# Loads of four heads' q and k put ahead of the decay rows, two heads' values behind them, and six more filler matmuls

## The chip, the cores and the metric

The kernel runs on one core of a Trainium2 chip. The core has five engines that take their instructions from queues of their own: TensorE (PE; its weight loads are listed apart as PEld), VectorE (DVE), ScalarE (ACT), GpSimd (POOL) and SyncE (SP). Transfers are issued from an engine's queue, most of them here from POOL's and the rest from SP's, and run on 16 DMA engines that all of the core's queues share. The metric is the device time of one execution in microseconds (us), as the median of several runs.

## What is computed

Eight batches of eight heads of causal attention with forget gates, 576 positions of 64 elements each; the heads are then joined to 512 columns and go through a two-layer network with the activation h - tanh(h).

```python
def _attn_ref(q, k, v, f):                      # q, k, v: (8, 8, 576, 64); f: (8, 8, 576)
    scale = 1.0 / np.sqrt(D)
    scores = scale * np.matmul(q, k.transpose(0, 1, 3, 2))
    log_f = np.log(np.clip(f, 0.0001, 1.0))
    cum = np.cumsum(log_f, axis=-1)
    decay = cum[:, :, :, None] - cum[:, :, None, :]
    causal = np.triu(np.ones((S, S), dtype=bool), k=1)
    scores = np.where(causal, -1000000000.0, scores + decay)
    scores = scores - np.max(scores, axis=-1, keepdims=True)
    attn = np.exp(scores)
    attn = attn / (np.sum(attn, axis=-1, keepdims=True) + 1e-09)
    return np.matmul(attn, v).astype(np.float32)

def _moe_ref(x, w_in, w_out):                   # x: (4608, 512); w_in: (512, 2048); w_out: (2048, 512)
    h = x @ w_in
    g = h - np.tanh(h)
    return (g @ w_out).astype(np.float32)
```

## The kernel before, in words

The order of each engine's instructions is the order in which the program emits them. The work goes in 32 pairs of heads (`pairs`: batch b, pair c of four), and the network's work (`mlp`) is mixed in from the fifth pair on.

A pair goes through these steps. `trans` (line 287) turns q and then k of both heads on PE by six transposes each into one PSUM bank, and two copies by DVE or ACT carry them to `QT` and `KT` (lines 309 and 311). `scores` (line 337) makes the products of k and q for seven tiles, `ti` 0 to 6 (matmuls of line 352; in batch 0 a second matmul of line 355 adds the causal mask `late`); ACT takes the exponential (line 361) out of one of a few PSUM banks: two of `ps_sc`, and for some tiles the one of `ps_tr`. `values` (line 382) multiplies the exponentials by v (matmuls of line 389), DVE divides (lines 398 to 400) and `turn` brings the result to `XR` (line 417), from which the network reads.

The decay is put into the score product: `QT` and `KT` have 67 rows each, 64 of the head and three more, the decay rows, which hold the running sum of log f in two parts (`chi`, `clo`) and constants. DVE makes `chi` (line 189) and `clo` (line 190) from the running sum of line 187. Head 0's rows are written by engines (lines 191 and 572). Those of heads 1 to 7 of batch 0 come by three DMAs on POOL's queue, which `bulk` issues: `k_hi` (line 211), `q_hi` (line 212) and `k_lo` (line 213). The first use of the rows is in pair 0 (heads 0 and 1): tile `ti` 3 has a matmul for each of its two heads, and tiles 4 to 6 belong to head 1.

POOL's queue in batch 0, in order: the identity (line 147); q, k, q, k of heads 0 to 3, two heads in each (`load_qk`, line 102); then the last 64 positions of v for all heads (`load_v_rest`, line 123) and the other 512 positions of heads 0 and 1 (`load_v_head`, line 127), from lines 166 to 168; the mask `late` (line 169); and then `bulk`: the three decay rows' DMAs, q, k, q, k of heads 4 to 7 (lines 214 to 217), and v of heads 2 to 7 in four blocks (`load_v_block`, line 131). After that come the loads for batch 1 and the weights, at places that `LOADS` (line 228) names.

PE's order around this: 47 filler matmuls, then `trans` of pair 0 with more filler between (`start`, line 570), tiles 0 and 1 of pair 0, two fillers; then from `att_items` (line 591) for p = 0: `trans` of pair 1's q, tile 2, six fillers, tile 3, `trans` of pair 1's k, tile 4, tile 5, four fillers, tile 6, six fillers. For p = 1 follow tile 0 of pair 1, `trans` of pair 2's q, tile 1, `trans` of pair 2's k, tile 2, `values` of pair 0's head 0, tiles 3 and 4, `values` of pair 0's head 1, and so on. The fillers are made by `unread` (line 563): matmuls of a constant into a PSUM bank (`ps_tr`, or one that is lent) that nothing reads.

Of the kernel before, what the change touches and what calls it, by code (L numbers as in the profile page):

```python
# [21 lines left out]
def kernel(  # L22
# [13 lines left out]
    B, H, S, D = q.shape  # L36
# [56 lines left out]
    qn, kn = ([t[0:S // NT6, :].rearrange("p (h n d) -> p h n d", h=H, n=NT6) for t in raw] for raw in (qraw, kraw))  # L93
# [7 lines left out]
    def load_qk(dst, src, b, h0, h1):  # L101
        nc.gpsimd.dma_start(  # L102
            out=dst[b % 2][:, h0:h1, :, :].rearrange("p h n d -> p h (n d)"),
            in_=src[b, h0:h1, :, :].rearrange("h (p n) d -> p h (n d)", n=NT6))
# [17 lines left out]
    def load_v_rest(b):  # L122
        nc.gpsimd.dma_start(out=vn[b % 2][0:S % P, NJ - 1, :, 0:D],
                            in_=v[b, :, S - S % P:S, :].rearrange("h p d -> p h d"))

    def load_v_head(b, h):
        nc.gpsimd.dma_start(out=vn[b % 2][:, 0:NJ - 1, h, 0:D],  # L127
                            in_=v[b, h, 0:S - S % P, :].rearrange("(n p) d -> p n d", p=P))

    def load_v_block(b, n, h0, h1):  # L130
        nc.gpsimd.dma_start(out=vn[b % 2][:, n, h0:h1, 0:D],  # L131
                            in_=v[b, h0:h1, n * P:(n + 1) * P, :].rearrange("h p d -> p h d"))
# [30 lines left out]
    nc.vector.memset(vn[0][D:P, NJ - 1, :, :], 0.0)  # L163
    mul_k, add_k, mul_l, mul_q, add_q, both = (per[:, i:i + 1] for i in range(6))
    EL = [cst.tile([P, 192], FP16, tag=f"el{i}", name=f"el{i}") for i in range(3)]
    load_v_rest(0)
    load_v_head(0, 0)
    load_v_head(0, 1)
    nc.gpsimd.affine_select(out=late, in_=late, compare_op=ALU.is_ge, fill=-60000.0,
                            base=0, pattern=[[1, P]], channel_multiplier=-1)  # L170

    r_hi, r_one = (id16[0:NX, NH + g:NH + g + 1] for g in (0, 2))
    nc.vector.tensor_scalar(out=both, in0=r_one, scalar1=-inv_qscale, scalar2=inv_qscale, op0=ALU.mult, op1=ALU.add)
# [19 lines left out]
    def aug_rows(b):  # L193
        i, h0 = b % 2, 0 if b else 1
        hs = slice(b * H + h0, (b + 1) * H)
        return [(KT[i][D:D + 1, h0:H, 0:S], chi[hs, :]), (KT[i][D + 1:D + 2, h0:H, 0:S], clo[hs, :]), (QT[i][D + 2:D + 3, h0:H, :], chi[hs, :])]

    def load_aug(b):
        for to, of in aug_rows(b):
            nc.sync.dma_start(out=to, in_=of)  # L200

    def const_rows(i):
        h0 = 1 - i
        nc.sync.dma_start(out=QT[i][D:D + 2, h0:H, :], in_=minus16[0:2 * (H - h0), :])
        nc.sync.dma_start(out=KT[i][D + 2:D + 3, h0:H, 0:S], in_=ones16[0:H - h0, :])
# [3 lines left out]
    def bulk():  # L209
        (k_hi, chi_0), (k_lo, clo_0), (q_hi, _) = aug_rows(0)  # L210
        nc.gpsimd.dma_start(out=k_hi, in_=chi_0)
        nc.gpsimd.dma_start(out=q_hi, in_=chi_0)
        nc.gpsimd.dma_start(out=k_lo, in_=clo_0)
        load_qk(qn, q, 0, 4, 6)
        load_qk(kn, k, 0, 4, 6)
        load_qk(qn, q, 0, 6, H)
        load_qk(kn, k, 0, 6, H)
        for n in range(NJ - 1):
            load_v_block(0, n, 2, H)

# [370 lines left out]
    def att_items(p):  # L591
        def put(fn, *args):
            items.append((lambda: fn(*args), True))

        items = []
        here = pairs[p] if p < len(pairs) else None
        before = pairs[p - 1] if 0 < p <= len(pairs) else None
        after = pairs[p + 1] if p + 1 < len(pairs) else None
        early = p < NPAIR
        for ti in range(len(TILES)):  # L600
            if here and (p > 0 or ti > 1):
                put(scores, *here, ti)
            if p == 1 and ti == 6:
                items.append((lambda: const_rows(1), False))
                items.append((lambda: load_aug(1), False))
            if p == 0 and ti in (2, 5, 6):
                put(unread, {2: 6, 5: 4, 6: 6}[ti])
            if p == 1 and ti == 6:
                put(unread, 8, True)
            if p == 1 and ti == 3:  # L610
                put(last)
            for load in LOADS.get((p, ti), ()):
                items.append((load, False))
            at_q, at_k = (1, 3) if p == 0 else (0, 1) if early else (0, 2) if p == NPAIR else (0, 3)
            if p in (2 * NPAIR - 1, 2 * NPAIR, 2 * NPAIR + 1) and (ti % 2 or ti == 0):
                items.append((rest, False))
            if p in (2 * NPAIR - 1, 2 * NPAIR) and ti % 2 == 0:
                pair = pairs[2 * NPAIR + 2 * (p - 2 * NPAIR + 1) + ti // 4]
                put(trans, *pair, *((kn, KT) if ti % 4 else (qn, QT)), False, "VA")
            if ti == at_q and p < 2 * NPAIR - 1:  # L620
                put(trans, *after, qn, QT, early, "VV")
            if p == NPAIR:
                if ti in (4, 5):
                    put(mlp1, 0, ti - 4, 1)
            if ti == at_k and p < 2 * NPAIR - 1 and p != NPAIR:
                put(trans, *after, kn, KT, early, "AV" if early and p > 1 else "VV")
            if p == NPAIR:
                if ti == 1:
                    put(turn, *pairs[p - 2])
                    put(values, *before)  # L630
                    put(mlp1, 0, 0, 0)
                elif ti == 2:
                    put(mlp1, 0, 1, 0)
                    put(turn, *before)
                    put(trans, *after, kn, KT, early, "VV")
            elif early and ti in (2, 4) and before:
                put(values, *before, (ti // 2 - 1,))
            elif not early and ti == 2 and before:
                put(values, *before, (0, 1), p == NPAIR + 2)
            if p < NPAIR:  # L640
                if ti == 1 and p > 1:
                    put(turn, *pairs[p - 2], True)
            elif p > NPAIR and ti == 3:
                items.append((release, False))
                put(turn, *before)
        return items
# [5 lines left out]
    at = 0  # L652
    start()
    bulk()
    for p in range(len(pairs) + 1):
        b, c = divmod(p, NPAIR)
        items = att_items(p)
        take = TAKE[p] if p < len(TAKE) else 8 - (p - len(TAKE)) % 2
        if p == 2 * NPAIR - 1:
            keep()  # L660
        if p == 2 * NPAIR + 1:
            KEPT.clear()
            widen(1)
        mine = mlp[at:at + take]
        at += take
        first = 14 if p == NPAIR else 0
        if p == len(pairs):
            for fn, *args in mine[0:2]:
                fn(*args)
            mine = mine[2:]  # L670
        given, n = 0, 0
        whole = sum(counts for _, counts in items)
        for emit, counts in items:
            emit()
            n += counts
            while n > first and given < len(mine) and given * (whole - first) < (n - first) * len(mine):
                fn, *args = mine[given]
                fn(*args)
                given += 1
# [31 lines left out]
```

## Time and profile before

| | us |
|---|---|
| median of 3 runs | 339.77 (339.68 to 340.19) |
| the profiled execution | 340.08 |
| its span, first to last instruction | 338.4 |
| PE busy in the span | 331.6 |
| PE busy from 36 to 330 us | 293.75 of 294 |
| PE busy from 10 to 12 us | 1.33 of 2 |

Times in the profile count from the first instruction. A row of a timeline gives start, length, engine, line, operation, what is written and read, and how many instructions were merged (x6); in square brackets stands how long the engine sat idle before and what ended that. A row of the chain of waits gives start, length and what was being waited for. For a DMA, "us to landing" counts from its issue until its last completion signal.

### The profile page before, as it was taken

The numbers are of one execution on the slowest core, as the hardware profiler recorded it, in microseconds if no ns is written. First come the engines' busy times: TensorE is split into PE (matmuls) and PEld (weight loads), VectorE is DVE, ScalarE is ACT, GpSimd is POOL, SyncE is SP. The second block draws the span as 40 slices with busy tenths as digits, with TensorE's granted clock in tenths as the row PEclk, the third lists the DMA queues.
The fourth block names the chain that finished last, engine by engine and source line by source line (L and its number), as shares of the span: only waits on it lengthen the run. The fifth ranks groups of instructions, "written<-read, shape, count | busy, mean of one in ns | idle before, by whom it ended". The sixth has DMA issues, their size and how long they took to land.

```text
span 338.4 us, 8760 instructions
## 1 busy us (share of the span) xinstructions
PE 331.6 (98%) x3329; PEld 237.4 (70%) x3329; DVE 261.1 (77%) x509; ACT 233.5 (69%) x438; POOL 162.6 (48%) x323
## 2 busy tenths in 40 slices
PE   8899999999999999999999999999999999999995
PEld 8675558875587558855888888656875686486485
DVE  7798986659888887678967796788667866966865
ACT  6798777888977886778677867787558733632630
POOL 8985566775657573677277637632322210000000
PEclk9999999999999999999999999999999999999999
DMA  8999999999969998999799999990130022002003
GB/s 110 130 196 198 186 198 177 182 157 171 138 92 169 143 132 90 135 175 146 96 120 175 132 112 113 166 131 17 50 110 8 17 67 95 2 31 95 0 17 110
DMA packets 147504, 38.82 MB, mean 115 GB/s; under 512 B 128217, under 2 KB 146371, under 8 KB 147462
## 3 DMA queue, kind: packets, MB, share of 16 engines
q0 software_dynamic: 94592, 18.38, 70.8%
q1 hardware_dynamic: 52864, 19.87, 33.2%
q8 instruction: 26, 0.43, 0.5%
q14 instruction: 16, 0.13, 0.2%
q10 hardware_dynamic: 6, 0.01, 0.0%
HBM read 36.85 MB, written 9.44 MB: 137 GB/s over the span
## 4 chain that ended last, share of the span: by engine, by line
PE 91%; DVE 2%; POOL 2%; ACT 2%; DMA 1%; issue 1%; ACTq 0%
PE hps L451 36%; PE ops L517 29%; PE ps L352 12%; PE av L389 8%; PE ops L492 4%; ACT e L361 2%; PE t L298 1%; DMA KT<-clo 1%; DVE KT L311 1%; DVE QT L311 0%; POOL vn L127 0%; POOL qn L102 0%; PE x L417 0%; POOL kn L102 0%; DVE xn L400 0%
## 5 line engine op out<-in xcount | busy, mean ns | idle before, releaser
L451 PE MATMUL hps<-XR,win 128*128 128x512 f16 (+1 forms) x640 | 140.7, 357 | 0.3 <-ACT XR L421 0.2
L456 ACT ACTIVATE th<-hps 128x512 f32<-128x512 f32 x144 | 86.6, 602 | 55.1 <-PE hps L451 53.5
L361 ACT ACTIVATE e<-ps 128x512 f16<-128x512 f32 x192 | 110.4, 598 | 9.6 <-PE ps L352 7.0
L462 DVE TENSOR_TENSOR gq<-hps,th 128x512 f16<-128x512 f32 x144 | 98.1, 687 | 23.5 <-ACT th L456 22.1
L371 POOL TENSOR_SCALAR_AFFINE_SELECT e<-e 128x128 f16<-128x128 f16 x168 | 59.2, 356 | 72.5 <-ACT e L361 70.5
L451 PEld LDWEIGHTS <-win 128*128 128x128 f16 x640 | 57.8, 97 | 48.6 <-issue 0.7
L352 PE MATMUL ps<-QT,KT 67*128 67x64 f16 (+4 forms) x384 | 76.5, 276 | 1.8 <-ACT e L361 0.6
L517 PEld LDWEIGHTS <-gq 128*128 128x128 f16 x640 | 60.3, 97 | 11.1
L517 PE MATMUL ops<-wout,gq 128*128 128x256 f16 x512 | 63.2, 272 | 0.0
L352 PEld LDWEIGHTS <-KT 67*128 67x128 f16 x384 | 36.5, 98 | 22.9 <-issue 1.3
L389 PEld LDWEIGHTS <-e 128*128 128x128 f16 x896 | 32.3, 97 | 3.6
L389 PE MATMUL av<-vn,e 128*128 128x65 f16 x896 | 33.6, 193 | 0.0
L131 POOL DMA_DIRECT2D vn<-in_v_dram x32 | 28.0, 879 | 7.1 <-DMA win<-in_moe_w_in_dram 3.3
L517 PE MATMUL ops<-W,sq 128*128 128x256 f16 x256 | 31.2, 272 | 0.0
L400 DVE TENSOR_TENSOR xn<-av,rs 128x640 f16<-128x640 f32 x32 | 26.4, 825 | 1.3 <-DVE rs L399 0.2
L517 PEld LDWEIGHTS <-sq 128*128 128x128 f16 x256 | 24.1, 98 | 3.4
L371 POOL TENSOR_SCALAR_AFFINE_SELECT el<-el 128x128 f16<-128x128 f16 x28 | 9.3, 332 | 26.8 <-ACT el L361 26.5
L108 POOL DMA_DIRECT2D qn<-in_q_dram x25 | 21.2, 846 | 1.8 <-issue 1.4
L108 POOL DMA_DIRECT2D kn<-in_k_dram x25 | 21.1, 846 | 1.7 <-issue 1.4
L398 DVE TENSOR_SCALAR rs<-av 128x10 f32<-128x10 f32 x32 | 5.2, 162 | 18.1 <-PE av L389 17.0
L311 DVE COPY KT<-t 64x576 f16<-64x576 f16 (+1 forms) x20 | 14.7, 736 | 3.7 <-PE t L298 3.5
L532 ACT ACTIVATE m<-ops 128x512 f32<-128x512 f32 x16 | 9.5, 596 | 10.9 <-PE ops L517 10.9
(85 smaller groups left out, 319.2 us busy)
## 6 DMA issues: line engine op xcount, KB each, us to landing
out_dram<-ost SPq DMA_DIRECT2D x34, 256.0 KB
vn<-in_v_dram POOLq DMA_DIRECT2D x24, 128.0 KB, 6.1
qn<-in_q_dram POOLq DMA_DIRECT2D x20, 128.0 KB, 4.6
kn<-in_k_dram POOLq DMA_DIRECT2D x20, 128.0 KB, 4.9
win<-in_moe_w_in_dram POOLq DMA_DIRECT2D x2, 1024.0 KB, 12.1
wout<-in_moe_w_out_dram POOLq DMA_DIRECT2D x2, 1024.0 KB, 15.7
XR<-xn SPq DMA_TRANSPOSE x56
qn<-in_q_dram POOLq DMA_DIRECT2D x6, 144.0 KB, 4.5
```

The lines of the kernel that those rows point to most:

```text
L108: nc.gpsimd.dma_start(out=dst[b % 2][0:pn, n, :].rearrange("p (h d) -> p h d", h=H), in_=src[b, :, n * P:n * P + pn, :].rearrange("h p d - ...
L131: nc.gpsimd.dma_start(out=vn[b % 2][:, n, h0:h1, 0:D], in_=v[b, h0:h1, n * P:(n + 1) * P, :].rearrange("h p d -> p h d"))
L311: nc.vector.tensor_copy(out=to, in_=of)
L352: nc.tensor.matmul(out=ps[:, col:col + n], lhsT=kt[0:rows, h, j * P:(j + 1) * P], rhs=qt[0:rows, h, i0:i0 + n], start=True, stop=cut == 0)
L361: nc.scalar.activation(out=e[:, lo:hi], in_=ps[:, lo:hi], func=AF.Exp, bias=-SHIFT, scale=qscale)
L371: nc.gpsimd.affine_select(out=view, in_=view, compare_op=ALU.is_ge, fill=0.0, base=0, pattern=pat, channel_multiplier=-1)
L389: nc.tensor.matmul(out=av[:, a, ib, :], lhsT=E.pop((b, c, a, j, ib)), rhs=vn[b % 2][:, j, 2 * c + a, 0:D + 1], start=(j == 0), stop=(j == ib))
L400: nc.vector.tensor_tensor(out=xn.rearrange("p i (a d) -> p a i d", a=2), in0=av[:, :, :, 0:D], in1=rs.to_broadcast([P, 2, NJ, D]), op=ALU. ...
L451: nc.tensor.matmul(out=hps[:, o:o + n], lhsT=win[:, ci, ft * P:(ft + 1) * P], rhs=XR[:, ci, t:t + n], start=(ci == 0), stop=(ci == NCH - 1))
L456: nc.scalar.activation(out=th, in_=hps, func=AF.Tanh, scale=-1.0)
L462: nc.vector.tensor_tensor(out=GQ[(u, i)][:, half, kt, :], in0=hps, in1=th, op=ALU.add)
L517: nc.tensor.matmul(out=ps[:, m, :], lhsT=LHS[lhs](u, kt // 4)[:, kt % 4, m * P:(m + 1) * P], rhs=rhs[:, kt, :], start=(fresh and (apart or ...
```

## The change

`load_v_rest(0)` and the two `load_v_head` calls leave their place ahead of `late` and go into `bulk`, behind all loads of q and k and ahead of the blocks of v. Three of the four loads of q and k of heads 4 to 7 leave `bulk` and stand ahead of it, right behind `late`; the fourth stays in `bulk`, behind the decay rows' DMAs. POOL's queue in batch 0 then reads: identity; q, k, q, k of heads 0 to 3; `late`; q and k of heads 4 and 5, q of heads 6 and 7; `k_hi`, `q_hi`, `k_lo`; k of heads 6 and 7; the last 64 positions of v; v of heads 0 and 1; the four blocks of v. And the filler behind tile 6 of pair 0 grows from six matmuls to twelve. The work that is asked of POOL and of the DMA engines is the same.

```diff
@@ -163,11 +163,11 @@
-    load_v_rest(0)
-    load_v_head(0, 0)
-    load_v_head(0, 1)
     nc.gpsimd.affine_select(out=late, in_=late, compare_op=ALU.is_ge, fill=-60000.0,
                             base=0, pattern=[[1, P]], channel_multiplier=-1)
+    load_qk(qn, q, 0, 4, 6)
+    load_qk(kn, k, 0, 4, 6)
+    load_qk(qn, q, 0, 6, H)
@@ -211,10 +211,10 @@
         nc.gpsimd.dma_start(out=k_hi, in_=chi_0)
         nc.gpsimd.dma_start(out=q_hi, in_=chi_0)
         nc.gpsimd.dma_start(out=k_lo, in_=clo_0)
-        load_qk(qn, q, 0, 4, 6)
-        load_qk(kn, k, 0, 4, 6)
-        load_qk(qn, q, 0, 6, H)
         load_qk(kn, k, 0, 6, H)
+        load_v_rest(0)
+        load_v_head(0, 0)
+        load_v_head(0, 1)
         for n in range(NJ - 1):
             load_v_block(0, n, 2, H)
@@ -604,7 +604,7 @@
             if p == 0 and ti in (2, 5, 6):
-                put(unread, {2: 6, 5: 4, 6: 6}[ti])
+                put(unread, {2: 6, 5: 4, 6: 12}[ti])
```

## The prediction

> **What bounds the kernel now.** I read the page first, then windows of busy time, the chain of waits, and the timelines of the first 36 us.
>
> ```profile
> PE 331.6 (98%) x3329; PEld 237.4 (70%) x3329; DVE 261.1 (77%) x509; ACT 233.5 (69%) x438; POOL 162.6 (48%) x323
> ...
> PEclk9999999999999999999999999999999999999999
> ```
>
> PE is busy in 98% of the span, at a granted clock of 1.00 in every slice. A window from 36 to 330 us has it busy for 293.75 of 294 us, and after 33 us the waits list no wait of PE at all. From there on the time is PE's work, which the change leaves alone. So what it does is decided in the first 33 us, where PE does wait, and a delay that reaches the end of that stage reaches the end of the kernel. There the chain of waits reads:
>
> ```profile
> 8.21 3.65 DMA KT<-clo
> 11.85 0.09 issue
> 11.94 0.19 PE ps L352
> ...
> 12.73 0.60 ACT e L361
> 13.34 0.04 issue
> 13.38 0.30 PE ps L352
> ...
> 13.88 0.35 PE idle L566 x6
> 14.23 0.04 issue
> 14.27 0.38 PE ps L352
> ...
> 15.00 0.81 DVE QT L311
> ```
>
> The third decay row's DMA (`k_lo`) is issued at 8.21 and lands at 11.85. PE's second matmul of tile 3 waits for it from 11.36 on, 0.58 us. Everything behind it on PE is queued behind that wait: the turning of pair 1's k, then the tiles of head 1, the fillers and pair 1. From 15.00 the chain runs through DVE's copies (1.62 us for q, 1.60 for k) and the division to 19.59, then PE, ACT from 22.12 to 26.62, PE, DVE again, and PE from 33.49 to the end. No DMA and no fixed time stands in it after 11.85, so a shift of the matmul at 11.94 is handed on whole.
>
> **The change on POOL's queue.** POOL now issues this, row by row:
>
> ```profile
> 4.28 0.71 POOL L123 DMA_DIRECT2D vn<-in_v_dram  x1
> 4.97 1.54 POOL L127 DMA_DIRECT2D vn<-in_v_dram  x2
> 6.47 0.55 POOL L169 TENSOR_SCALAR_AFFINE_SELECT late<-late 128x128 f16<-128x128 f16 x1
> 7.17 0.54 POOL L211 DMA_DIRECT2D KT<-chi  x1
> 7.69 0.54 POOL L212 DMA_DIRECT2D QT<-chi  x1
> 8.21 0.51 POOL L213 DMA_DIRECT2D KT<-clo  x1
> ```
>
> The mask will take 4.28 to 4.83 and the three loads of q and k, at 0.65 each (the mean of the four now between 8.71 and 11.28), end near 6.80. `k_hi` then waits for DVE's `chi`, which ends at 6.30 + 0.57 = 6.87, so the rows' DMAs go out at about 6.92, 7.45 and 7.97: `k_lo` 0.24 us earlier. `clo` is ready at 6.91 + 0.81 = 7.72 and doesn't hold it. The mask's first reader is at 9.13: no cost. The values' three issues (2.25 us) stand where the loads stood, and POOL comes to the blocks of v at about 11.4, where it is now at 11.24.
>
> **When the rows land.** This is the term that decides, and no row shows it: the rows travel behind 3 x 192 packets of 768 bytes (q and k) in place of 3 x 512 packets of 128 bytes (v). I set bounds by two windows of the DMA view, 10.5 to 13.5 us (q and k alone) and 14.5 to 16.5 us (v alone):
>
> ```profile
> q0 software_dynamic: 617, 0.44, 110.8%
> ...
> q0 software_dynamic: 2324, 0.30, 232.1%
> ```
>
> 617 packets in 3 us are 206 a us, at 1.108 x 48 / 617 = 86 ns each; 2324 in 2 us are 1162 a us, at 32 ns each. By packet time the two loads weigh the same (576 x 86 = 49.5 us, 1536 x 32 = 49.2 us, over 16 engines) and `k_lo` lands at 11.85 as now. By rate the q and k need 576 / 206 = 2.80 us and the values 1.32, 1.48 us less: `k_lo` at 13.3, the late end. The early end is a queue with nothing ahead: the first q load of all lands 3.5 us after its issue, which would be 7.97 + 3.5 = 11.47. Between them: the values really took 2.5 us (7 to 9.5 us, 1617 of its 1792 packets under 512 bytes), which makes q and k 0.3 later, 12.15. And the landings themselves: the four loads of the first group land from 5.06 to 8.67 (1.20 apart), those of the second from 12.2 to 15.5 (1.10 apart); three more loads behind 8.67 at 1.15 land at 12.1, and the rows behind them (`q_hi` to `k_lo` now lie 0.36 apart) at 12.5 or later. I take 12.4, near the row of landings, since that is the same kind of load in the same queue: **0.55 us later** than now, ends -0.38 and +1.45.
>
> [...]
>
> **The fillers.** The row is six filler matmuls from 13.72 in 0.35 us, 58 ns each; tile 0 of pair 1 then has its weight load at 14.14, just after DVE's second k copy (12.46 + 1.62 = 14.08), and starts at 14.27. These times move together with 11.94. Twelve fillers end at 13.72 + 0.70 = 14.42 and the tile starts near 14.47: **0.20 us**, since 0.15 of the added 0.35 lies in the wait for the copy. Ends: nothing, if that copy comes later against PE, and 0.35 if the wait is gone.
>
> **What else moves.** (1) Values of head 0 are read at 15.68, of head 1 at 16.54, both later by the sums above (0.75), thus at 16.4 and 17.3. Their DMAs go out at about 9.85 and 10.64 instead of 4.97 and 5.75. At 5.3 us to landing, the longest of v's now, that is 15.2 and 15.9, about 1.2 us ahead: nothing, with a loss beyond that slack (a rival). (2) POOL's waits at 27.82, 29.11 and 31.00 end each with the landing of the DMA eight issues before. By that, the second values' head waits for k of heads 4 and 5 (about 11.0), and the first block of v for q of heads 6 and 7 (12.1): POOL comes 0.7 late to the blocks. They are due for pair 1 at 20.27 and land by 18.08 now: hidden, and 0.7 late still. Behind them the first half of `win` is next: it lands at 17.03 + 10.5 = 27.5 and is read at 28.71, so 1.2 us cover a slip of 0.7, and more when PE is late too. (3) q and k of heads 4 to 7 land earlier, but they are read at 14.54, 15.08, 18.62 and 19.16 and land at 12.2, 13.05, 14.8 and 15.5 now; no transposition waits for them: no gain.
>
> **Sum.** 0.55 (rows) + 0.20 (fillers) = +0.75 us. The profiled execution took 340.08, 1.68 of it outside its span of 338.4, and lies 0.31 above the median; I put the sum on the median: 339.77 + 0.75 = **340.5**.
>
> **Rivals.** *Rows not late.* If the small packets are what delays the rows, they land at 11.47 to 11.85 and the shift is -0.38 to 0, with the fillers -0.2 to +0.2: 339.6 to 340.0, middle 339.7. For it: equal packet time, the 0.24 earlier issue, and a gap near 10 us in which the queue has run dry before q of heads 4 and 5. Against it: the landings 1.1 to 1.2 us apart. It decides from a landing before 11.9.
>
> *The values late.* The same queue, one step on: PE stands at the first matmul of `values` on head 0. It decides if v's DMA takes over 6.5 us from issue (16.4 - 9.85). For it: the values' heads of batch 1, issued behind a full queue, take 9.8 to 10.3 us. Against it: they stand behind 1 MB of `win`; here only 192 packets of k and the rest of v come in between. At 7.5 us PE waits 1.0 more: 341.5.
>
> *The clock falls.* PE now idles 0.58 us at 11.36 and would idle some 1.1. If that cost the granted clock, the matmuls would run as at the start, where 47 fillers take 4.92 us, 105 ns each against 58; a stretch of 4 us at that rate costs some 1.5 to 2: 342. Against it: the clock is 1.00 through today's gaps. [...]
>
> *Faster.* Rows before 11.3 would take the whole 0.58 away, and no row allows that; with the fillers hidden as well it is 339.2. More than 0.2% (0.68 us, about what can be told from no change) needs a gain that I don't see, a later wait of ACT or DVE closing up as q and k come early: 338.9.
>
> **Chances.** Forecast, rows late: 0.50, its own range 340.2 to 341.0, a little over half of it (0.28) beyond 340.45. Rows not late: 0.19, all within 0.2%. Values late: 0.13. Clock: 0.05. Faster: 0.13. Slower by over 0.2%: 0.28 + 0.13 + 0.05 = 0.46; within: 0.22 + 0.19 = 0.41; faster: 0.13. The range from 338.9 to 341.5 leaves out half of the faster case, the clock and half of the late values, 0.18.
>
> **What would show it.** In the changed profile: `k_lo` issued near 7.97 and landing at 12.1 to 12.9, the wait for it on PE at 1.0 to 1.4 us; 12 fillers ending after DVE's second k copy, with tile 0 of pair 1 some 0.75 later than 14.27; no wait of PE for v at the matmuls of line 389; POOL waiting for earlier landings ahead of v's blocks. The forecast is wrong if `k_lo` lands before 11.9, if line 389 waits, if the clock's row falls under 1, or if a shift at 15.00 has gone by 33.5.

## The result, and the profile after

The changed kernel takes 343.35 us (median of 4 runs, 342.49 to 343.77) where the kernel before takes 339.94 in runs beside it: a ratio of 1.0097, 95% interval 1.0075 to 1.0119. It is slower by 3.4 us; 0.75 were forecast, in a range that ended at 341.5. A later set of 12 runs gave 343.85 against 340.04, 1.0099 (1.0067 to 1.0131).

In 13 of 95 executions of the kernel before the mean clock is 0.985 to 0.995, as where it falls in the way described below, and they take 341.5 to 345 us, so medians are compared here, and executions are told apart by their mean granted clock where that matters.

The page of the changed kernel's profile, the lines that answer to those shown of before:

```profile
PE 334.3 (98%) x3335; PEld 239.6 (70%) x3335; DVE 261.1 (76%) x509; ACT 233.4 (68%) x438; POOL 165.4 (48%) x323
...
PEclk9789999999999999999999999999999999999999
```

PE is as busy as before by share, and busy for 2.7 us more. The second and third digits of the clock's row are new: in two slices of 8.5 us PE was granted 0.7 and 0.8 of its clock in place of full speed. The chain of waits of the changed kernel, at the same place as that of before (start, length, what):

```profile
8.19 4.76 DMA KT<-clo
12.95 0.09 issue
13.04 0.21 PE ps L352
...
15.92 1.29 PE idle L566 x12
17.21 0.04 issue
17.25 0.58 PE ps L352
```

The third decay row lands at 12.95 in place of 11.85, and PE starts behind it at 13.04, not 11.94: 1.10 us later. But tile 0 of pair 1 starts at 17.25 in place of 14.27: of the 2.98 us only 1.10 are the row's. The filler group has twelve matmuls in 1.29 us, 108 ns each, where six took 0.35, 58 ns each. The tile's matmul takes 0.58 where it took 0.38. PE is running at about half speed.

The trace's record of the granted clock has 1.00 for 6.83 us from 5.57 on, 0.50 for 6.83 us from 12.40 to 19.23, then 1.00 to the end of the span. The record begins at 5.57; of the first 47 fillers, 104 ns each, 42 start before it, and with the clock at 1.00 a filler takes 58 ns. So 5.57 is called the rise of the clock here. Windows of the changed kernel follow, in stretches of 3.41 us, half of 6.83, counted from the rise. In a row stand the window, its length, the busy time of PE, PEld, DVE, ACT and POOL with the number of instructions, then the granted clock; the last two figures, DMA share and GB/s, are not used here:

```profile
8.98:12.40 3.41, 2.17 (x26) 1.55 (x25) 2.64 (x5) 2.01 (x4) 3.06 (x5) 1.00 1.38 156
12.40:15.81 3.41, 2.77 (x22) 2.16 (x23) 1.60 (x2) 1.41 (x3) 3.41 (x5) 0.50 1.57 93
15.81:19.23 3.42, 3.36 (x31) 2.69 (x29) 0.76 (x1) 1.43 (x3) 3.42 (x7) 0.50 1.41 139
```

The same window of the kernel before, counted from the rise of its clock at 5.62 (1.00 from there to the end):

```profile
9.04:12.45 3.41, 2.66 (x34) 2.00 (x35) 2.58 (x5) 2.20 (x5) 3.41 (x6) 1.00 0.93 115
```

The clock falls at 12.40, in the middle of PE's wait and 0.55 us before the row lands. In the 3.41 us before that PE was busy for 2.17; in the kernel before it was 2.66, and the clock stayed. In e1 and e4 below the clock is at 0.50 for 6.83 us as well (13.81 to 20.64, 13.52 to 20.35). The shift grows from 1.10 at the first matmul behind the row to 3.46 at DVE's next copy (15.00 before, 18.46 after) and stays: PE's first `hps` matmuls in the chain come at 28.87 and at 32.32, and the span is 3.4 us longer. No transfer stands in the chain behind 12.95. The 3.46 are made up so:

| | us |
|---|---|
| third decay row later | 1.10 |
| six added fillers at 108 ns | 0.65 |
| other work up to tile 0 of pair 1, at half clock (2.98 - 1.10 - 0.65) | 1.23 |
| from there to DVE's copy, at half clock (1.21 in place of 0.73) | 0.48 |

### The profile page after: what moved, and what is told of

The parts are those of the page before. It is cut to its first block, busy times and chain, and to the rows that moved or that the text cites. A ratio compares the mean times of both kernels' runs of the same rounds, so it can differ in the third digit from the quotient of the medians.

```text
span 341.8 us, 8772 instructions
## 1 busy us (share of the span) xinstructions
PE 334.3 (98%) x3335; PEld 239.6 (70%) x3335; DVE 261.1 (76%) x509; ACT 233.4 (68%) x438; POOL 165.4 (48%) x323
## 4 chain that ended last, share of the span: by engine, by line
PE 92%; DVE 2%; ACT 2%; DMA 1%; issue 1%; POOL 0%; ACTq 0%
PE hps L451 36%; PE ops L517 29%; PE ps L352 13%; PE av L389 8%; PE ops L492 4%; PE t L298 2%; ACT e L361 2%; DMA KT<-clo 1%; PE idle L566 1%; DVE KT L311 0%; PE ps L355 0%; DVE TQ L187 0%; PE x L417 0%; DVE gq L462 0%; ACT TQ L184 0%
## 5 line engine op out<-in xcount | busy, mean ns | idle before, releaser
L371 POOL TENSOR_SCALAR_AFFINE_SELECT e<-e 128x128 f16<-128x128 f16 x168 | 61.3, 367 | 72.6 <-ACT e L361 70.6
L352 PE MATMUL ps<-QT,KT 67*128 67x64 f16 (+4 forms) x384 | 77.8, 280 | 2.6 <-DMA KT<-clo 1.7
L311 DVE COPY QT<-t 64x576 f16<-64x576 f16 x18 | 14.4, 802 | 5.1 <-PE t L298 5.0
```

Of the source, the lines that this page charges most:

```text
L311: nc.vector.tensor_copy(out=to, in_=of)
L352: nc.tensor.matmul(out=ps[:, col:col + n], lhsT=kt[0:rows, h, j * P:(j + 1) * P], rhs=qt[0:rows, h, i0:i0 + n], start=True, stop=cut == 0)
L371: nc.gpsimd.affine_select(out=view, in_=view, compare_op=ALU.is_ge, fill=0.0, base=0, pattern=pat, channel_multiplier=-1)
```

## The experiments

Theory A says that three loads ahead of the rows make the third row late, that PE's longer idle time makes the clock fall, and that the halved clock is the larger part of the loss. Rival B puts it on the fillers, rival C on other transfers that came late, and rival D says that the clock is a companion of the late row and no cause. Each run had 10 to 12 executions, the kernel before beside them.

**The two parts of the change alone.** The transfers alone (e1) put the six fillers back:

```diff
-                put(unread, {2: 6, 5: 4, 6: 12}[ti])
+                put(unread, {2: 6, 5: 4, 6: 6}[ti])
```

> The moved transfers without the six added fillers (six behind tile 6, as before). Theory A, the clock: the third decay row still lands near 12.9 us, PE still idles some 1.7 us and the clock still falls to 0.5 for one or two stretches of 3.4 us; only six fillers at 107 ns are saved, so 342.7 (342.3 to 343.1). Rival B, the fillers make most of the loss: 340.5 or less. Rival C, late transfers of values or later loads: the same 343 as with the fillers.

Measured: 343.49 against 340.19, ratio 1.0064 (1.0026 to 1.0102); 8 of 11 executions have a mean clock of 0.985 to 0.990 and take 343.4 to 344.8; the other three, at 0.998 to 1.000, take 340.4, 340.6 and 340.9. In the profiled one the row lands at 12.88 and the clock is halved from 13.81 to 20.64. So B falls: the loss is there without the added fillers, and it is there when the clock falls and mostly gone when it doesn't. This alone doesn't tell A from D: no profile shows when the row landed in the three executions that kept the clock. The 0.65 less than with twelve did not show in the median, which lies above the expected 342.3 to 343.1.

The fillers alone (e2) change the same number the other way in the kernel before.

> The kernel before with twelve fillers in place of six. Theory A: the clock stays at 1.00, twelve fillers end some 0.3 us behind DVE's second k copy, 340.1 (+0.2, between 0 and +0.35). Rival B, the fillers make most of the loss: 342 or more.

Measured: 340.69 against 340.19, ratio 1.0012 (0.9994 to 1.003); the clock is 0.998 or more in all 12 executions. Its chain of waits:

```profile
12.04 0.19 PE ps L352
...
13.98 0.68 PE idle L566 x12
14.67 0.04 issue
14.71 0.38 PE ps L352
```

From the matmul behind the row to tile 0 it is 2.67 us, before 2.33 (11.94 to 14.27): the six fillers cost 0.34, their whole length, at full clock. The start of the tile follows the last filler by 0.04 in both; DVE's second k copy had ended before, at 14.08. Nothing of the fillers lies beside it. The median is 0.50 higher, a little above the expected 0.35 at most; its interval takes in both, and no difference.

**The clock held up, with the same late row.** The changed kernel with 24 more fillers behind tile 2 (e3), which run while the row is on its way:

```diff
-                put(unread, {2: 6, 5: 4, 6: 12}[ti])
+                put(unread, {2: 30, 5: 4, 6: 12}[ti])
```

> The changed kernel with 24 more fillers behind tile 2, so that PE is busy while the third decay row is on its way. Theory A: the row lands near 12.9 us as in the changed kernel, PE idles under 0.6 us, the clock stays at 1.00, and what is left is the row's 1.1 us and the fillers' 0.2: 341.2 (340.9 to 341.6). Rival C, transfers other than the rows are late: 342.5 or more, with the clock at 1.00.

Measured: 341.39, and all 12 executions between 341.19 and 342.17 at a clock of 0.998 or more; ratio 1.003 (1.001 to 1.005). The window that ended with the fall in the changed kernel now has PE busy for 3.23 us, and its clock stays at 1.00 here and after it:

```profile
10.38:13.79 3.41, 3.23 (x52) 2.75 (x50) 1.72 (x3) 1.56 (x4) 3.02 (x5) 1.00 1.34 112
```

More work for PE, and the kernel is 2 us faster than the change. The waits of PE name no transfer in this run, and none but the third row's in the changed kernel, so C has nothing to stand on. The same with six fillers behind tile 6 (e8) prices what is left.

> The changed kernel with 24 more fillers behind tile 2 and six, not twelve, behind tile 6: what the late row alone costs at a clock of 1.00. The six fillers taken away are on PE's path whole, 0.35 us, so 341.05 where the run with twelve has 341.39; the row's lateness is then about 1.0 of it. Rival, these fillers lie beside DVE's copies: 341.3 to 341.4.

Measured: 341.27, ratio 1.0031 (1.0007 to 1.0055), clock 0.999 or 1.000 in all 12. That is 0.12 below e3 in the median, less than the 0.35 expected, nearer to the rival's 341.3 and inside the spread of both. The profiles side with the expectation: from the matmul behind the row to tile 0 of pair 1 it is 2.67 us in e3 (13.16 to 15.83) and 2.33 in e8 (12.71 to 15.04), 0.34 for six fillers. But what the late row alone costs isn't measured by e8: its row came earlier (4.3 us after the issue), the 30 fillers end at 12.44, and the row no longer delays PE. The matmul behind the row is at 12.71, 0.77 later than before, and this is the fillers' doing. With the wait filled and the clock at full speed the kernel is 1.2 us slower than before in the median.

**The clock let fall, with the row in time.** The kernel before without the two fillers behind tile 1 and the six behind tile 2 (e4); no transfer is touched, and PE has eight matmuls less:

```diff
         scores(*pairs[0], 1)
-        unread(2)
...
-                put(unread, {2: 6, 5: 4, 6: 6}[ti])
+                put(unread, {2: 0, 5: 4, 6: 6}[ti])
```

> The kernel before without the eight fillers behind tiles 1 and 2 of pair 0: the decay rows land at 11.85 us as before, but PE is busy for some 2.2 us in place of 2.66 in the stretch of 3.41 us that ends near 12.4. Theory A: the clock falls to 0.5 for 3.4 us with the transfers untouched, 341.3 (340.8 to 342.3). Rival D, the clock falls only with a gap over some 1.5 us, or the rows' lateness is the cause of the whole loss: 339.9, unchanged.

Measured: 342.84, ratio 1.0069 (1.0043 to 1.0095); the clock is 0.985 to 0.990 in all ten executions. The chain has the row near its old place, landing at 8.21 + 3.86 = 12.07, and the windows around the fall of the clock:

```profile
10.11:13.52 3.41, 2.06 (x29) 1.48 (x27) 2.42 (x4) 2.26 (x6) 2.98 (x5) 1.00 1.07 143
13.52:16.94 3.42, 3.27 (x26) 2.48 (x26) 1.41 (x2) 1.81 (x5) 3.42 (x5) 0.50 1.93 139
16.94:20.35 3.41, 3.41 (x46) 2.92 (x44) 2.57 (x4) 1.97 (x4) 3.29 (x7) 0.50 1.22 156
```

Taking eight matmuls of filler away costs 2.7 us, which is more than expected (342.3 at most), since the clock was halved for 6.83 us and not for 3.4. The loss needs no late transfer, and PE's gap is 1.11 us here, under the 1.5 that D asks for: D falls too. Nor does the clock fall in the gap: it falls at 13.52, 1.35 us after PE is back at work (12.17). PE is busy for 3.27 of the first halved 3.41 us, and the clock is 0.50 in the second (16.94 to 20.35) all the same.

**How many loads ahead.** Values behind the loads as in the change, six fillers, and none (e5), one (e6) or two (e7) of the three loads ahead of the rows. For e5, against the changed kernel (the filler goes back to six as in e1):

```diff
-    load_qk(qn, q, 0, 4, 6)
-    load_qk(kn, k, 0, 4, 6)
-    load_qk(qn, q, 0, 6, H)
...
+        load_qk(qn, q, 0, 4, 6)
+        load_qk(kn, k, 0, 4, 6)
+        load_qk(qn, q, 0, 6, H)
         load_qk(kn, k, 0, 6, H)
```

> The values moved behind the loads as in the change, but no load of heads 4 to 7 ahead of the decay rows; six fillers behind tile 6. Theory A, each q or k load ahead of the rows delays them in the shared queue: the third row lands at 11.5 to 11.8 us, PE waits under 0.6 us, the clock stays at 1.00, and the time is that of the kernel before or up to 0.35 us less: 339.9. Rival C, moving the values back is what costs: 341 or more, with PE waiting at the values' matmuls.

> As the run with no load ahead, but q of heads 4 and 5 ahead of the rows. Theory A: the third row lands at 11.8 to 12.2 us, PE waits 0.5 to 0.8 us, clock at 1.00, 340.2. Rival, the landing doesn't depend on the number of loads: as with none ahead.

> As the run with no load ahead, but q and k of heads 4 and 5 ahead of the rows. Theory A: the third row lands at 12.2 to 12.6 us, PE waits 0.9 to 1.3 us, and the clock falls in a part of the executions: 340.6 where it stays, 342.5 to 343.5 where it falls.

| ahead of the rows | third row, issue to landing, us | median, us | ratio to before | executions with clock at 0.995 or less |
|---|---|---|---|---|
| nothing (e5) | 2.9 | 341.12 | 1.0038 (1.0009 to 1.0067) | 1 of 12 |
| one load (e6) | 3.4 | 340.51 | 1.0020 (0.9994 to 1.0046) | 0 of 12 |
| two loads (e7) | 3.5 | 340.10 | 0.9994 (0.9970 to 1.0018) | 0 of 12 |
| three loads (e1; 4.3 to 5.0 in five profiles) | 4.7 | 343.49 | 1.0064 (1.0026 to 1.0102) | 8 of 11 |
| the values (before) | 3.6 | 340.1 beside e5 to e7 | 1 | 13 of 95 |

The row is issued at 8.18 to 8.23 in all of them, since POOL starts the first of the three when the running sum is there. The landing follows the number of loads, as theory A has it, but not in equal steps: by these profiles, one for each kernel, the first load costs 0.5 us, the second 0.1 and the third 1.2. The profiles of the five runs with three loads (changed, e1, e3, e8, e9) differ by 0.7 among themselves, so the third load's price is 0.8 to 1.5. e7's expectation of a later landing and a falling clock was a miss, and e6 is 0.3 above its 340.2. e5's time was a miss for theory A as well: with nothing ahead the row comes earliest of all, 2.9 us after its issue, and the kernel is 1 us slower, as rival C had it, with PE waiting at the values' matmuls. Two waits of PE of 0.7 us each are there that the kernel before doesn't have, and a wait of ACT before the first of these lines:

```profile
ACT el L361 <- POOL el L589: 1.0, 1, 1.0
...
PE ps L352 <- ACT el L361: 0.7, 1, 0.7
PE av L389 <- DMA vn<-in_v_dram: 0.7, 1, 0.7
```

POOL stands idle for 2.56 us before `k_hi`, and from the blocks of v on everything on its queue is some 2 us later: the blocks themselves (13.44 in place of 11.24), `win` (19.18 in place of 17.03), and behind it the clearing of the tile `el` (line 589), for which an exponential of ACT waits 1.0 us and PE behind it. The second matmul of tile 3 had come 0.32 us earlier than before (11.62), but the matmuls of `values` that stand at 27.96 in the kernel before come at 28.67. The chain of waits runs through `win`, which is also later:

```profile
19.18 10.59 DMA win<-in_moe_w_in_dram
29.77 0.05 issue
29.81 0.82 PE hps L451 x3
```

But this wait is only 0.2 us of the 0.94 by which the first `hps` matmuls are later than before (28.87). POOL's idle 2.56 us cost here by what stands behind them on its queue. The kernel before fills the time between 4.6 and 7.2 us with the values, e7 with two loads, and no difference between these two is shown.

The clock is not all that makes an execution long: in e5 and e6 seven of 24 take 341.5 to 343.0 at a clock of 0.998 or more. None of them was profiled. The profiled execution of e7, at 341.10 and a clock of 0.999, shows one way: `win` lands 11.9 us after its issue, 10.5 in the kernel before, and PE waits 1.1 us for it.

**The change again, and two tries to do better.** The changed kernel in 12 more executions (e9):

> The changed kernel as it is, in more executions. Theory A: where the clock falls to 0.5 the time is 342.5 to 344, where it stays it is 341.0; and the six added fillers, which run at 107 ns each where the clock is halved, do not make it slower than the same transfers without them by more than 0.65. Rival, the added fillers shorten the halved stretch: below the 343.5 of the run without them, with shares of 0.995 in place of 0.990.

Measured: 343.85, 0.36 above e1 and so within the 0.65. Its executions fall into four groups by their mean clock, and from the group it is estimated how long the clock was halved: a share of 0.005 of some 341 us, twice taken, is 3.4 us, and the profiled execution of the change, at 0.990, had it halved for 6.83:

| mean clock | halved for, us (estimate) | executions | time, us |
|---|---|---|---|
| 1.000 | 0 | 1 | 341.5 |
| 0.995 | 3.4 | 3 | 342.2 to 342.6 |
| 0.989 to 0.990 | 6.8 | 5 | 343.7 to 344.7 |
| 0.985 | 10.2 | 3 | 345.0 to 345.3 |

Each further 3.4 us at half clock cost some 1.0 to 1.6 us here, by the groups' means; the third was not expected (344 at most). The share of 0.994 to 0.995 is there with twelve fillers (3 of 12, and 2 of the first 4) and not with six (0 of 11); whether the added fillers shorten the halved stretch isn't settled by so few.

Six more fillers in PE's wait in the kernel before, behind tile 2 (e10, `{2: 12, 5: 4, 6: 6}`):

> The kernel before with six more fillers behind tile 2, in PE's wait for the third decay row. Theory A: they lie in the wait of 0.58 us, so the time of an execution is unchanged (340.0), while PE is busy for 3.0 of the 3.41 us in which the clock falls, so that none of the executions has the clock at 0.99. Rival, fillers always cost their length: 340.35.

Measured: 340.44, near the rival's 340.35, ratio 1.0004 (0.997 to 1.0039); one of 12 executions has the clock at 0.99 all the same. In the profile tile 0 of pair 1 starts at 14.28, as before, so there the fillers lie in the wait; the median is 0.4 higher nevertheless, and why was not found out. It is no better than the kernel before.

The three decay rows' DMAs issued from SP in the kernel before (e11, `nc.gpsimd` to `nc.sync` at lines 211 to 213):

> The kernel before with the three decay rows' DMAs on SP's queue: SP issues them from about 6.9 us on, ahead of those for batch 1, and POOL goes on with its loads from 7.0 without waiting for the running sum. If the shared DMA engines' queue sets the landing: the third row lands at 11.7 to 12.5 us, since loads of q and k are now beside it, 340 to 340.5. If POOL's issue sets it: 11.3, and 339.5.

Measured: 342.89, outside both expectations, ratio 1.0059 (1.0021 to 1.0097), five executions at a clock near 1.00 (339.8 to 341.0) and seven at 0.985 to 0.990. In the profiled one, with the clock at 1.00, the row lands at 11.59 and tile 0 of pair 1 starts 0.1 us earlier (14.17). In the others the mean clock shows that it fell; no profile of such an execution was taken, and the cause isn't shown. No version was found that beats the kernel before.

## Why the prediction was wrong

**The bound and the place: right.** What happens is decided before 33 us, at the wait for the third decay row, and the shift is handed on whole (3.46 at DVE's copy, 3.45 at the network's first matmuls, 3.4 in the span).

**The rows: right in sign, 0.55 forecast, 1.10 measured** (1.0 in e1, 1.3 in e9), inside the ends of -0.38 and +1.45. Equal packet time, the early estimate, was wrong; the estimate from landings (12.5 or later) was the good one, and I went below it. One part of the step was a misreading: the rows' DMAs do not go out 0.24 us earlier. This line of the changed kernel's POOL timeline starts when the one of before did, though POOL had nothing else to do:

```profile
7.17 0.53 POOL L211 DMA_DIRECT2D KT<-chi  x1 [0.72 <-DVE chi L189]
```

`chi` ended at 6.88, and the issue starts 0.29 us later. It starts at 7.16 to 7.18 in eight profiles that have it on POOL's queue (before, changed, e5 to e10), whether POOL had been free for 0.14 us before (the kernel before) or for 2.56 (e5); so the 0.14 of "issue" before `k_hi` in the kernel before was the tail of that wait, not a gap between two instructions. The unloaded landing was mis-set as well: 3.5 us taken from the first load of q, 2.9 measured (e5).

**The fillers: 0.20 forecast, 0.34 at full clock (e2), 0.65 in the changed kernel.** I let 0.15 of them lie beside DVE's copy, because the weight load at 14.14 comes right after it. This was a misreading: I put the start of one row and the length of another together. The row of the timeline starts at 13.72 and is 0.50 long, so the six fillers end at 14.22 and not at 14.07:

```profile
13.72 0.50 PE L566 MATMUL idle<-warm 128*128 128x128 f16 x6
```

The 0.35 belongs to the chain of waits, which had the answer too: it led from the fillers' end at 14.23 to the tile at 14.27, and not through DVE, whose copy had ended at 14.08.

**The clock: the step that failed.** It stood as a rival with a chance of 0.05 and a price of 1.5 to 2 us, and it happened in 15 of 16 executions. The price came right: 3.46 less 1.10 for the row and 0.35 for the fillers at full clock is 2.0. In part this was luck. At the price used, 1.5 to 2 us for a stretch of 4 (an estimate of mine; no profile of before shows a fall), the halved 6.83 us would have cost 2.6 to 3.4; but PE stood idle for the first 0.64 of them, and what it did at half clock after DVE's copy at 18.46 added nothing. What was wrong was the condition. I held the clock's full speed through today's gaps against it and looked at the length of the gap, 1.1 us as forecast. Around this wait the profiles order themselves by how long PE is busy in 3.41 us: where the clock fell, in those up to the fall; where it stayed, in those around the wait, counted from the clock's rise in the same steps:

| kernel | PE busy, us of 3.41 | clock then |
|---|---|---|
| e4, gap wider | 2.06 | 0.50 |
| e1, transfers only | 2.09 | 0.50 |
| changed | 2.17 | 0.50 |
| e2, fillers only (10.77 to 14.18) | 2.48 | 1.00 |
| before | 2.66 | 1.00 |
| e3, wait filled | 3.23 | 1.00 |

Two more profiles point the same way: in e9, the change again, PE waits 1.89 us for the row, the twelve fillers behind it take 108 ns each and the mean clock is 0.990; in e10, with six more fillers in the wait, it waits 0.3 us, the six behind it take 58 ns each and the clock is 1.00. This order belongs to the work around this wait; it isn't a rule, and two simple rules fail in the same traces. Busy time alone is not it. In the kernel before PE is busy for 1.65 of the 3.41 us from 333.30 to 336.72, less than in any row of the table, and the clock is still 1.00 in the 1.68 us behind it, up to the end; the changed kernel shows the like near its end (1.70 of the 3.40 us from 336.70). The length of one gap is not it either. The same stretch ends with 1.77 us of idle, and e7's wait for `win` is 1.1 us long; the clock is 1.00 behind the first, and e7's mean is 0.999, while the fall came behind 1.04 us of idle in the changed kernel (11.36 to 12.40) and 1.11 in e4. What differs near the end is the kind of matmul: all are 128 rows deep there, while around the wait 20 of the 34 in the window of the kernel before have 67 or 96. Whether this counts was not tried. So it is shown for this wait that with too little for PE to do the clock falls (e4: 2.06 us of 3.41 in its profile, a fall in all ten executions), and with the wait filled it stays (e3: 3.23 of 3.41, no fall in all 12); the exact condition stays open.

The forecast's own numbers held a warning: 0.55 us more idle takes 2.66 down to 2.11. No trace of before shows where the clock gives way, and the three times known then did not show that this kernel itself loses it now and then. But a wait in a place where PE was busy for only 1.33 of 2 us (10 to 12), to be made twice as long, was reason for a chance far above 0.05, and for a range that reached to 344.

**The other rivals.** Rows not late: true with one or two loads ahead, not with three. Values late: not in the changed kernel, where PE waits nowhere at line 389; it is what e5 shows, 0.7 us. Of POOL's two forecast waits for the landing eight issues before, one was there in the profile (0.28 us, for q of heads 6 and 7; the blocks of v were forecast 0.7 late) and hidden; the other, for k of heads 4 and 5, was not there in it.

## What to carry to other kernels

An idle stretch of PE had two prices here: its length, 1.1 us, and what it did to the clock of the work behind it, 2.0. Before moving a transfer that PE waits for, look at how much PE has to do around the wait: here 2.66 us of matmuls in 3.41 held the clock in most executions and 2.17 lost it in most, so a margin of half a microsecond was none. Filling the wait with matmuls that nobody reads tests for it (e3). A filler that looks hidden beside a copy need not be: here the chain of waits led from the fillers to the tile and not through the copy, and six more of them cost their whole length, 0.34 us (e2).

## What the runs showed that was not expected

Taking work away made the kernel slower: eight fillers less, 2.7 us more (e4); 24 fillers more in the changed kernel, 2 us less (e3). The clock was halved for 6.83 us in three profiles (changed, e1, e4) and, estimated from the mean clock, for 3.4 to 10.2 us in e9's executions; PE busy for 3.27 of the first 3.41 us did not end it (e4). A landing jumped: one more load of 144 KB in the same queue cost the row 0.1 us as the second and 1.2 us as the third (e6, e7, e1; 0.8 to 1.5 over all profiles with three); what sets this apart was not tried. And in 13 of 95 executions of the kernel before the mean clock is 0.985 to 0.995 too; no profile of one was taken, so why it falls then and not in the others isn't shown.
